# A sliding-window attention block and a mixer MLP on one core: the warm-up reads a tile of zeros, the q and k weights come as two loads, block 3's second norm takes bn_stats, and the whole order is written anew

## The chip, the core and the metric

The kernel runs on one core of a Trainium2 chip, in bf16 with f32 accumulation. The metric is the device time of one launch in microseconds (us). Engines are named as in the profile: PE (TensorE), DVE (VectorE), ACT (ScalarE), POOL (GpSimd) and SP (SyncE, which issues every DMA here).

## The reference, cut to what matters

```python
# S = 2048 rows, D = 448, H = 16 heads of 28, F = 1792
y  = x + A(layernorm(x), wqkv, wo)          # attention
h2 = y + B(layernorm(y), w1, w2, w3, w4)    # mixer and MLP; B normalises its input once more
def A(x, wqkv, wo):
    q, k, v = split(x @ wqkv)               # each row looks at 8 rows: pos, pos-2, ..., pos-14
    logits = einsum("bhsd,bhswd->bhsw", q, k[idx]) * scale      # masked where pos < 0
    return einsum("bhsw,bhswd->bhsd", softmax(logits), v[idx]) @ wo
def B(x, w1, w2, w3, w4):
    h  = gelu(layernorm(x) @ w1)
    hs = concat(4 column groups of h, shifted by +1, -1, +2, -2 rows) @ w2
    x1 = x + hs
    return x1 + gelu(layernorm(x1) @ w3) @ w4
```

## The kernel before

The 2048 rows are four **blocks** of 512 (t = 0 to 3), each of four tiles of 128 rows. The functions `phase_*` record operations, in program order, with the reads and writes of each; nothing is emitted then. Block by block they are:

- **N1**: the first norm. `ln_stats` gives `bn_stats` and `bn_aggr` on DVE (with `STATS` 'a' instead: sums on ACT, by a Copy and a Square that also write out an accumulated sum); `rstd` gives Ln and Exp on ACT; `normalize` writes `lntm`.
- **A1**: the normalised tiles are transposed into `actT` (block 0 by PE transposes against the identity `ident`, tile after tile, in `transposed_single`; later blocks also by DMA), then q and k are computed transposed. `duo` runs two output banks at once on the two halves of the PE rows. The six column groups go in three pairs. **V**: the values, in `vt`, and DMAs that window them into `vw`.
- **A2** and **S**: four products q times shifted k on DVE (`qk_r`: three of 128x4096, one of 128x2048), summed over a head's columns by PE (`zc`), then the softmax: max, subtract, Exp, sum, Ln and Exp for the reciprocal, and `pb`, which PE transposes and ACT copies to `pt` in the arena.
- **A3** and **O**: four products `bd_r` on DVE spread the weights, PE multiplies them with `vw`, copies go to `actT`, and PE multiplies with `wo`; the residual sum replaces `xin`.
- **B1** and **M**: the second norm (twice normalised, so two reciprocal roots), a DMA transpose ("turn"), `w1` and gelu into `gT`.

Then, by units of 2, 4, 4, 4 and 2 tiles: **B2** (`w2` on shifted `gT`, sum on DVE, statistics), **T** (normalise, turn, add x), **W3** (`w3` and gelu, `h3T`) and **B3** (`w4`, sum, store).

What runs when is not decided by these functions. `ORDER` is a list of operation numbers; `arrange` walks it, hands out buffers from small pools (8 PSUM banks, 2 of `qk_r`, 3 of `bd_r`, 4 of `actT`, 2 of `lntm`), and so gives each engine its own queue, which runs strictly in that order. `OTHER` names operations that go to their alternative engine (a copy from ACT to DVE, an addition from POOL to DVE). Waits follow from the recorded reads and writes. ACT holds one table of functions at a time: going from Ln and Exp to gelu or back costs an ACT_TABLE_LOAD in its queue.

Ahead of the data, `warm` gives PE nine matmuls of `ident` with itself; `keep_busy` puts two more between the first transposes. `ident` needs a memset and an affine_select on POOL. In the profile nearly all operations have line L1048 (before) or L1051 (after), where the queues are emitted, so the tile names tell them apart.

## Time and profile before

| what | us |
|---|---|
| median of 3 runs | 189.56 |
| lowest and highest | 188.63, 190.37 |
| the profiled execution | 188.72 |
| its span in the trace | 187.0 |
| PE busy | 180.0 |
| DVE busy | 130.8 |
| ACT busy | 124.0 |

The span begins with the first instruction of the trace and ends with the last; the 1.72 us around it lie outside the trace. Every time given for an instruction is counted from the span's start. A timeline row gives start, length, engine, operation, what is written from what, the count, and in brackets the idle time before it with what ended it. Matmuls are pipelined, so a matmul's length is longer than its share of PE; its share is the distance between starts.

### The profile page before, as it was taken

Reading aid. Unit: us, or ns where it says so; the run is one execution under the profiler, and the core shown is the slowest. Engines: PE = TensorE matmul, PEld = TensorE weight load, DVE = VectorE, ACT = ScalarE, POOL = GpSimd, SP = SyncE. Lnnn points to the kernel's source line nnn. Section 1 sums busy time; section 2 is a strip of 40 time slices with the busy share of each in tenths; the row PEclk is TensorE's granted clock in tenths of the full one; section 3 lists DMA queues with packets and bytes.
Section 4 is the critical chain, followed back from the end, with each engine's and each line's share of the span. In section 5 each row is a group of like instructions: output and inputs, shape, how many; then the busy total and the mean of one; then the engine's idle time right before and its main releaser. Section 6 shows DMA issues by size and latency. Waiting matters only on the chain.

```text
span 187.0 us, 5742 instructions
## 1 busy us (share of the span) xinstructions
PE 180.0 (96%) x2482; PEld 93.5 (50%) x2482; DVE 130.8 (70%) x236; ACT 124.0 (66%) x280; POOL 20.9 (11%) x56
## 2 busy tenths in 40 slices
PE   5999999989999989999999999999999999999994
PEld 2685443345453445467455444555444544555663
DVE  7989999999999999999997960089962080000512
ACT  4459989879999999998991987930267004930340
POOL 3440000000003000500042000020034050000000
PEclk9999999999999999999999999999999999999999
DMA  5923583661654697597409060043305031000022
GB/s 151 340 101 58 125 173 63 141 149 17 115 124 94 160 206 301 100 316 146 101 4 140 2 137 4 0 31 84 100 4 112 4 71 60 4 0 0 4 98 74
DMA packets 38609, 18.29 MB, mean 98 GB/s; under 512 B 27464, under 2 KB 38072, under 8 KB 38584
## 3 DMA queue, kind: packets, MB, share of 16 engines
q1 hardware_dynamic: 38584, 17.93, 41.4%
q8 instruction: 19, 0.31, 0.7%
q14 instruction: 6, 0.05, 0.1%
HBM read 8.14 MB, written 1.84 MB: 53 GB/s over the span
## 4 chain that ended last, share of the span: by engine, by line
PE 75%; DVE 16%; ACT 6%; issue 1%; POOL 0%; POOLq 0%
PE ps L1048 75%; DVE bd_r L1048 6%; DVE qk_r L1048 4%; DVE lntm L1048 2%; ACT lntm L1048 1%; DVE xin L1048 1%; DVE st L1048 1%; ACT arena L1048 1%; DVE mx L1048 1%; ACT h3T L1048 1%; ACT L1048 1%; ACT L1043 1%; DVE arena L1048 1%; ACT xin L1048 1%; DVE pb L1048 0%
## 5 line engine op out<-in xcount | busy, mean ns | idle before, releaser
L1048 PE MATMUL ps<-actT,arena 64*128 64x512 bf16 (+2 forms) x812 | 69.6, 326 | 0.3
L1048 ACT ACTIVATE h3T<-ps 128x512 bf16<-128x512 f32 (+1 forms) x70 | 30.7, 520 | 39.1 <-PE ps L1048 38.7
L1048 PEld LDWEIGHTS ps<-actT,arena 64*128 64x128 bf16 (+1 forms) x812 | 35.7, 96 | 29.8 <-PE ps L1048 1.6
L1048 PE MATMUL ps<-arena,h3T 64*128 64x448 bf16 (+3 forms) x434 | 44.5, 343 | 0.0
L1048 DVE SCALAR_TENSOR_TENSOR ost<-ps,mrs,arena 128x448 bf16<-128x448 f32 (+2 forms) x17 | 10.7, 649 | 35.5 <-PE ps L1048 26.9
L1048 ACT ACTIVATE arena<-ps 128x512 bf16<-128x512 f32 (+4 forms) x62 | 31.5, 568 | 2.6 <-PE ps L1048 2.4
L1048 DVE TENSOR_TENSOR qk_r<-arena 128x4096 bf16<-128x4096 bf16 (+1 forms) x16 | 32.1, 2015 | 0.3 <-PE ps L1048 0.3
L1048 PEld LDWEIGHTS ps<-arena,h3T 64*128 64x128 bf16 (+1 forms) x434 | 22.4, 94 | 19.6 <-ACT h3T L1048 0.3
L1048 DVE TENSOR_TENSOR bd_r<-arena,bmask 80x2048 bf16<-80x2048 bf16 x16 | 18.9, 1211 | 0.3 <-ACT arena L1048 0.3
L1048 DVE TENSOR_SCALAR lntm<-arena,mv,rs_y 128x512 bf16<-128x512 f32 x14 | 6.8, 540 | 13.1 <-ACT rs_y L1048 11.6
L1048 POOL TENSOR_TENSOR arena<-arena,xin 128x448 f32<-128x448 f32 x9 | 10.6, 1193 | 34.3 <-DVE lntm L1048 34.3
L1048 PE MATMUL ps<-wo_s,actT 64*128 64x448 bf16 x128 | 14.3, 350 | 0.1
L1048 PE MATMUL ps<-w_s,arena 64*128 64x448 bf16 x88 | 13.3, 350 | 0.0
L1048 PE MATMUL ps<-actT,w_s 64*128 64x512 bf16 (+1 forms) x112 | 13.3, 376 | 0.0
L1048 ACT ACTIVATE lntm<-xin,nm 128x448 bf16<-128x448 bf16 x16 | 10.5, 660 | 4.0 <-DVE nm L1048 4.0
L1048 ACT ACTIVATE actT<-ps 128x512 bf16<-128x512 f32 (+2 forms) x19 | 11.8, 639 | 2.0 <-PE ps L1048 1.9
L1048 PE MATMUL ps<-arena,actT 64*128 64x448 bf16 x112 | 12.6, 350 | 0.1
L1048 DVE SCALAR_TENSOR_TENSOR arena<-xin,rs_y,ps 128x448 f32<-128x448 bf16 x16 | 10.3, 673 | 0.3 <-PE ps L1048 0.3
L1048 DVE BATCH_NORM_STATS2 st<-xin 128x6 f32<-128x448 bf16 x16 | 9.1, 612 | 0.5 <-DMA xin<-in_A_x_dram 0.4
L1048 ACT ACTIVATE vt<-ps 128x448 bf16<-128x448 f32 x16 | 8.4, 543 | 1.0 <-PE ps L1048 1.0
L1048 PEld LDWEIGHTS ps<-wo_s,actT 64*128 64x128 bf16 x128 | 5.9, 94 | 6.1 <-PE ps L1048 0.9
L1048 PEld LDWEIGHTS ps<-actT,w_s 64*128 64x128 bf16 (+1 forms) x112 | 6.0, 98 | 5.6 <-ACT h3T L1048 0.2
(75 smaller groups left out, 167.1 us busy)
## 6 DMA issues: line engine op xcount, KB each, us to landing
arena<-in_B_w_dram SPq DMA_DIRECT2D x2, 896.0 KB, 7.0
out_dram<-ost SPq DMA_DIRECT2D x15, 112.0 KB, 1.8
arena<-in_B_w_dram SPq DMA_DIRECT2D x2, 784.0 KB, 5.8
vw<-vt SPq DMA_DIRECT2D x4, 320.0 KB, 4.1
vw<-vt SPq DMA_DIRECT2D x4, 256.0 KB, 3.5
arena<-in_A_wqkv_dram SPq DMA_DIRECT2D x2, 448.0 KB, 4.5
xin<-in_A_x_dram SPq DMA_DIRECT2D x2, 448.0 KB, 5.1
xin<-in_A_x_dram SPq DMA_DIRECT2D x3, 224.0 KB, 5.3
```

The costliest lines, as they stand in the source:

```text
L1043: eng.preload_act_table_set("natural_log_exp_and_others")
L1048: inst = getattr(eng, meth)(**kw)
```

## The change

1. POOL first sets a new tile `blank` to zero, and the warm-up and keep-busy matmuls read it in place of `ident`. There are ten warm-up matmuls in place of nine.
2. The load of the q and k columns of `wqkv` (2 DMAs of 448 KB) becomes q, then k (4 DMAs of 224 KB). In block 0 the pairs of column groups are (q0,q1), (k0,k1), (q2,k2) in place of (q0,k0), (q1,k1), (q2,k2).
3. Block 3's second norm takes its sums by `bn_stats` on DVE in place of sums with the residual addition on DVE and Squares on ACT.
4. `ORDER` and `OTHER` are new. By the new `OTHER`, three of block 0's four `actT` copies run on DVE (one before), the two `actT` copies of block 3's attention that ran on DVE go back to ACT, and one addition of unit 2 goes back to POOL.

```diff
-STATS = {'N1': 'vvva', 'B1': 'avaa', 'B2': 'avvvv'}
+STATS = {'N1': 'vvva', 'B1': 'avav', 'B2': 'avvvv'}
...
 OTHER = """
-103 196 198 510 513 564 565 627 629 699 700 701 769 830
+107 110 112 201 203 572 573 637 638 706 709 779 838
 """
-WARM = 9
+WARM = 10
...
+        blank = sb("blank", [128, 128], BF16)
...
+        pool("memset", ap=blank[:], constant=0.0)
         pool("memset", ap=ident[:], constant=0.0)
...
-        load_rows("wqk", wqkv_s[:, :, 0:2 * D], A_wqkv, 0, 2 * D)
+        load_rows("wq", wqkv_s[:, :, 0:D], A_wqkv, 0, D)
+        load_rows("wk", wqkv_s[:, :, D:2 * D], A_wqkv, D, D)
...
-            return mm(busy(), ident[:], bass.AP(ident, 0, [[128, 128], [0, 4], [1, 128]]), True, True, 512, after)
+            return mm(busy(), blank[:], bass.AP(blank, 0, [[128, 128], [0, 4], [1, 128]]), True, True, 512, after)
...
-            names = ("q0", "k0", "q1", "k1", "q2", "k2")
+            names = ("q0", "k0", "q1", "k1", "q2", "k2") if t else ("q0", "q1", "k0", "k1", "q2", "k2")
```

The new `ORDER` moves instructions on every engine. Three places on DVE, as its queue stands in the built programs:

The head of DVE's queue before, from the last setup memset ahead of the first tile: `st<-xin` are the statistics of x, `lntm<-xin` the normalised tiles of block 0, `actT<-ps` the copy of a transposed tile, `vt` and `pb` setup memsets.

```order
L1048 MEMSET pb 128x320
L1048 BN_STATS st<-xin 128x6
L1048 BN_AGGR mv<-st 128x2
L1048 BN_STATS st<-xin 128x6
L1048 BN_AGGR mv<-st 128x2
L1048 TENSOR_SCALAR lntm<-xin,mv,rs_y 128x448
L1048 BN_STATS st<-xin 128x6 x2
L1048 BN_AGGR mv<-st 128x2 x2
L1048 TENSOR_SCALAR lntm<-xin,mv,rs_y 128x448
L1048 MEMSET vt 128x128x2
L1048 TENSOR_SCALAR lntm<-xin,mv,rs_y 128x448 x2
L1048 COPY actT<-ps 128x512
```

And the same place in the changed kernel, up to the statistics of block 1:

```order
L1051 MEMSET vt 128x128x2
L1051 BN_STATS st<-xin 128x6
L1051 BN_AGGR mv<-st 128x2
L1051 BN_STATS st<-xin 128x6
L1051 BN_AGGR mv<-st 128x2
L1051 BN_STATS st<-xin 128x6 x2
L1051 BN_AGGR mv<-st 128x2 x2
L1051 TENSOR_SCALAR lntm<-xin,mv,rs_y 128x448 x4
L1051 COPY actT<-ps 128x512 x3
L1051 MEMSET pb 128x320
L1051 BN_STATS st<-xin 128x6 x2
```

All four tiles' statistics now stand ahead of the first normalised tile, three copies stand where one stood, and the two memsets have changed places.

DVE at the end of block 0's softmax, before: `qk_r` are block 1's products, `ls`, `mx` and `pb` the softmax, `bd_r` the first product of block 0's A3, which needs `pb` transposed by PE and copied by ACT.

```order
L1048 TENSOR_TENSOR ls<-ps,mx 128x512
L1048 TENSOR_TENSOR qk_r<-arena 128x4096
L1048 TENSOR_SCALAR lntm<-xin,nm,rs_y 128x512
L1048 TENSOR_REDUCE mx<-ls 128x64
L1048 TENSOR_SCALAR lntm<-xin,nm,rs_y 128x512 x3
L1048 TENSOR_TENSOR pb<-ls,mx 128x8x64
L1048 TENSOR_TENSOR qk_r<-arena 128x2048
L1048 TENSOR_TENSOR bd_r<-arena,bmask 80x2048
```

The same place in the changed kernel:

```order
L1051 TENSOR_TENSOR ls<-ps,mx 128x512
L1051 TENSOR_SCALAR lntm<-xin,nm,rs_y 128x512 x4
L1051 TENSOR_REDUCE mx<-ls 128x64
L1051 TENSOR_TENSOR qk_r<-arena 128x2048
L1051 TENSOR_TENSOR pb<-ls,mx 128x8x64
L1051 TENSOR_TENSOR qk_r<-arena 128x4096
L1051 TENSOR_TENSOR bd_r<-arena,bmask 80x2048 x2
```

A wide product now stands between `pb` and the first `bd_r`, where a narrow one stood, and four normalisations in place of a wide product stand ahead of the sum over `ls`.

DVE around block 3's A3, before: `st<-arena` are unit 1's statistics, `lntm<-arena` its four normalised tiles (their turn feeds W3 of unit 1), `bd_r` block 3's products, CAST its copies.

```order
L1048 TENSOR_TENSOR pb<-ls,mx 128x8x64
L1048 BN_STATS st<-arena 128x6 x3
L1048 TENSOR_TENSOR bd_r<-arena,bmask 80x2048 x2
L1048 BN_AGGR mv<-st 128x2 x4
L1048 TENSOR_TENSOR bd_r<-arena,bmask 80x2048
L1048 TENSOR_SCALAR rs_x<-mv 128x4
L1048 CAST actT<-ps 128x512
L1048 TENSOR_TENSOR bd_r<-arena,bmask 80x2048
L1048 TENSOR_SCALAR lntm<-arena,mv,rs_y 128x512 x4
L1048 CAST actT<-ps 128x512
```

The same place in the changed kernel:

```order
L1051 TENSOR_TENSOR pb<-ls,mx 128x8x64
L1051 BN_STATS st<-arena 128x6 x2
L1051 BN_AGGR mv<-st 128x2 x4
L1051 TENSOR_SCALAR rs_x<-mv 128x4
L1051 TENSOR_TENSOR bd_r<-arena,bmask 80x2048 x3
L1051 TENSOR_SCALAR lntm<-arena,mv,rs_y 128x512
L1051 TENSOR_TENSOR bd_r<-arena,bmask 80x2048
L1051 TENSOR_SCALAR lntm<-arena,mv,rs_y 128x512 x3
```

All of unit 1's statistics now stand ahead of the first `bd_r`, and the two casts are gone from DVE. On ACT, both copies of block 3's `pb` now stand behind the Ln and Exp of block 2's second norm (one stood ahead of the Ln before), and on PE its transposes stand behind two groups of B3's matmuls where they stood behind one.

60 rows, old and new, of the table ORDER are left out of this document.

## The prediction

> **What bounds the kernel now.** I read the page first, then the busy times by stretch, then the chain that ended last, and last the timeline where the stretches change.
>
> ```profile
> span 187.0 us, 5742 instructions
> PE 180.0 (96%) x2482; PEld 93.5 (50%) x2482; DVE 130.8 (70%) x236; ACT 124.0 (66%) x280; POOL 20.9 (11%) x56
> PE   5999999989999989999999999999999999999994
> DVE  7989999999999999999997960089962080000512
> PEclk9999999999999999999999999999999999999999
> ```
>
> PE looks full and DVE looks idle for a third of the span, but these are averages over two stages: DVE is full up to slice 21 (about 98 us) and loose behind it. The stretches say where the change of hands lies (a row gives the length, then the busy time of PE, PEld, DVE, ACT and POOL, each with its count, the granted clock and the DMA).
>
> ```profile
> 40.00:67.80 27.80, 26.27 (x588) 13.07 (x590) 27.73 (x37) 26.07 (x64) 1.53 (x3) 1.00 0.53 108
> 67.80:85.39 17.59, 17.25 (x239) 9.75 (x240) 17.45 (x33) 17.13 (x38) 2.61 (x3) 1.00 0.74 222
> 85.39:100.00 14.61, 14.61 (x288) 8.33 (x290) 13.30 (x25) 12.49 (x25) 3.29 (x3) 1.00 0.49 97
> 100.00:140.00 40.00, 40.00 (x396) 19.05 (x392) 25.82 (x66) 22.52 (x46) 2.96 (x6) 1.00 0.30 52
> 140.00:184.96 44.96, 44.57 (x480) 24.48 (x476) 9.81 (x17) 15.39 (x35) 5.00 (x4) 1.00 0.17 41
> ```
>
> From 40 to 67.8 us DVE idles 0.07 us and PE 1.53: **DVE decides**. From 67.8 on PE idles 0.34 us, then nothing, and 0.39 in the last stretch: **PE decides**. The last real waits of PE are these two, for block 2's A3 product and for block 0's gelu:
>
> ```profile
> 66.96 0.42 PE L1048 MATMUL ps<-bd_r,vw 80*32 80x64 bf16 x32 [0.52 <-DVE bd_r L1048]
> 67.78 0.35 PE L1048 MATMUL ps<-w_a,arena 64*128 64x448 bf16 x1 [0.40 <-ACT arena L1048]
> ...
> 85.39 99.20 PE ps L1048 x1158
> ```
>
> The last row is from the chain: one unbroken run of PE, 99.2 us long, ends the kernel. The new order puts the same matmuls ahead of that point as the old one (all of block 0 to 2's attention, B2 of units 0 and 1, W3 of unit 0) and the same behind it. So the result is a sum of two terms: by how much DVE's queue comes earlier or later to 67 us, and what PE newly waits for behind it.
>
> **The head.** PE first, then DVE:
>
> ```profile
> 2.09 4.02 PE L1048 MATMUL ps<-ident 128*128 128x512 bf16 x9 [2.09 <-POOL ident L1048]
> 5.91 0.63 PE L1048 MATMUL ps<-ident,lntm 128*128 128x128 bf16 x4
> 7.61 0.86 PE L1048 MATMUL ps<-ident,lntm 128*128 128x128 bf16 x8
> 8.40 5.32 PE L1048 MATMUL ps<-actT,arena 64*128 64x256 bf16 x100
> 2.19 0.99 SPq L1048 DMA_DIRECT2D arena<-in_A_wqkv_dram  x2
> 1.39 0.20 POOL L1048 MEMSET ident<- 128x128 bf16 x1
> ...
> 2.47 0.33 DVE L1048 MEMSET pb<- 128x320 uint32 x1
> 2.90 0.63 DVE L1048 BATCH_NORM_STATS2 st<-xin 128x6 f32<-128x448 bf16 x1
> 4.29 0.18 DVE L1048 BATCH_NORM_AGGREGATE mv<-st 128x2 f32<-128x6 f32 x1
> 4.41 0.40 DVE L1048 TENSOR_SCALAR lntm<-xin,mv,rs_y 128x448 bf16<-128x448 bf16 x1
> 6.36 0.27 DVE L1048 MEMSET vt<- 128x256 uint32 x1
> 6.68 1.10 DVE L1048 TENSOR_SCALAR lntm<-xin,mv,rs_y 128x448 bf16<-128x448 bf16 x2
> 7.70 0.41 DVE L1048 COPY actT<-ps 128x512 bf16<-128x512 bf16 x1
> 8.52 0.63 DVE L1048 BATCH_NORM_STATS2 st<-xin 128x6 f32<-128x448 bf16 x1 [0.41 <-DMA xin<-in_A_x_dram]
> ```
>
> The warm-up waits for `ident`. With `blank` as POOL's first instruction (0.20 us from 0.80, where POOL's first memset starts) PE begins at about 1.05 us, 1.04 earlier. Nine warm matmuls took 5.91 - 2.09 = 3.82, so ten take 4.25, to 5.3. That alone moves nothing: before, the first tile was normalised by 4.81 (4.41 + 0.40) and waited 1.1 us for PE to leave the warm-up. Now DVE does the statistics of all four tiles first. From 4.47, where the second aggregate ends, two more bn_stats with overlap (1.15), two aggregates (0.30) and one normalisation (0.40) give 6.2. The wait has changed sides: PE idles from 5.3 to 6.2, and the transposes start 0.3 later than at 5.91. The split load adds two DMA issues of 0.5 us (0.99 for two) ahead of block 1's x, which landed at 8.5; at worst it lands at 9.5, the same as the late end below. The first matmuls that read a weight start at 8.40 and read q alone.
>
> What counts is when DVE gets to block 1's statistics, 8.52 before. Its queue now holds two more copies of 0.41; `vt` (0.27) has moved into the free time ahead of 2.90, and `pb` (0.33) has moved out of it, ahead of block 1. The third and fourth transposes bind the copies. How late depends on PE's rate, which doubles in this stretch: 0.42 us for 512 columns in the warm-up, but 5.32 / 50 = 0.106 for 256 (two at once) from 8.40. The granted clock reads 9 (90% or more) throughout, so only the distances show it. The doubling came by about 8.1, six us after PE's first matmul. If it stays at 8.1, the four transposes and two keep-busy matmuls at the old rate end at about 8.6, copies run to 9.2, `pb` to 9.5: block 1's statistics are **0.9 late**. If it comes before 6.2, the last normalisation binds instead: the pair that took 1.10 us from 6.68 now starts about 0.2 earlier and ends at 7.6, copies end at 8.7, `pb` at 8.85: **0.3 late**. Six us after PE's first matmul would now be 7.1, and by that I take **+0.5**.
>
> The Trainium skill ("TensorE: Matmul & The Clock Gate", Part 1) says that PE starts at half clock and goes to full after one busy window of about 3.4 us, and that the windows run freely. The trace agrees with the halves (0.42 against 0.21 for 512 columns) and not with the page's other figure, about 4 us into activity: here it was 6. By the window, the rate would double anywhere between 4.5 and 7.9 (an estimate from that page), and the term would be +0.3 to +0.9, the same bounds.
>
> **The order up to 67 us.** DVE's work from block 1's statistics to block 2's residual sum is the same list of operations. What differs are its idle times:
>
> ```profile
> 11.61 1.31 DVE L1048 TENSOR_SCALAR lntm<-xin,mv,rs_y 128x448 bf16<-128x448 bf16 x4 [0.60 <-ACT rs_y L1048]
> 21.25 3.43 DVE L1048 TENSOR_TENSOR qk_r<-arena 128x4096 bf16<-128x4096 bf16 x2 [0.26 <-PE ps L1048]
> 25.09 0.17 DVE L1048 TENSOR_SCALAR nm<-mv 128x4 f32<-128x4 f32 x1 [0.42 <-ACT lntm L1048]
> 25.17 2.29 DVE L1048 TENSOR_TENSOR qk_r<-arena 128x4096 bf16<-128x4096 bf16 x1
> 35.48 1.22 DVE L1048 TENSOR_TENSOR qk_r<-arena 128x2048 bf16<-128x2048 bf16 x1
> 37.03 1.22 DVE L1048 TENSOR_TENSOR bd_r<-arena,bmask 80x2048 bf16<-80x2048 bf16 x1 [0.33 <-ACT arena L1048]
> 15.99 0.60 SPq L1048 DMA_DIRECT2D xin<-in_A_x_dram  x1
> ```
>
> The first wait (0.60) stays: statistics, Ln and Exp, normalisation follow each other as before. The one at 21.25 was a wait for a product buffer whose matmuls stood far back in PE's queue; they now start when the second product ends, before the third needs the buffer: gone. The one at 25.09 waited for block 3's sums on ACT, whose x came by a DMA that SP issued at 15.99 behind a halo copy; that load now goes out with the others, and ACT has these sums earlier in its queue: gone. The one at 37.03 was the way from `pb` through PE and ACT to the first `bd_r`, covered by a narrow product of 1.22 us; a wide one of 2.29 covers it now, so it is gone. Together 1.01. New waits can come where four normalisations now stand ahead of the sum over `ls`, which needs ACT's Exp: walking ACT's queue with its own rows I find the Exp done within 0.1 to 0.3 of when DVE gets there. I take **-0.8**, with -1.0 (all gone) and 0 (all come back elsewhere) as the ends.
>
> **Behind 67 us.** The extra matmul is in the head. Block 3's statistics: four Squares leave ACT, four bn_stats and aggregates come to DVE:
>
> ```profile
> 102.83 0.67 ACT L1048 ACTIVATE lntm<-xin,nm 128x448 bf16<-128x448 bf16 x1 [3.84 <-DVE nm L1048]
> L1048 DVE BATCH_NORM_STATS2 st<-xin 128x6 f32<-128x448 bf16 x16 | 9.1, 612 | 0.5 <-DMA xin<-in_A_x_dram 0.4
> 89.49 2.33 DVE L1048 TENSOR_TENSOR bd_r<-arena,bmask 80x2048 bf16<-80x2048 bf16 x2
> 97.45 1.98 SPq L1048 DMA_TRANSPOSE actT<-lntm  x1
> 103.01 10.75 PE L1048 MATMUL ps<-actT,arena 64*128 64x512 bf16 x98
> 107.94 1.89 SPq L1048 DMA_TRANSPOSE actT<-lntm  x1
> ```
>
> Squares cost 4 x 0.65 = 2.6 us on an ACT that had idled 3.84; bn_stats and aggregates cost DVE about 4 x 0.53 + 0.4 = 2.5 with overlap, two of them while the last residual sums wait for PE. The turn that follows went out at 107.94; I get 107.4 for the new one. PE has W3 of unit 1 to do from 103.01 for 10.75 us, so this is worth **0** either way; without that cover it would be the 0.5. The addition given back to POOL and the casts given to ACT lie beside full PE too.
>
> The tight place is W3 of unit 1 at 103.01: its turn went out at 97.45. In the new order block 3's `pb` is transposed one B3 group later (14 matmuls, about 1.3 us), and both copies stand behind a table load, so the first `bd_r` starts at about 90.7 in place of 89.49, and DVE idles about 0.9 ahead of it. DVE no longer does two casts there, and the fourth normalisation of unit 1 ends at about 97.0, 0.4 before the old one. So **0** again, with +0.6 as the end if the copies on ACT come late for O.
>
> **Sum:** +0.5 - 0.8 + 0 + 0 = -0.3 on the profiled execution's 188.72 us (span 187.0 and 1.72 around it): 188.4. That execution was 0.84 under the median 189.56, so on the median the forecast is **189.3**; its own range, from the bounds, is +0.9 + 0 + 0.6 = +1.5 and +0.3 - 1.0 = -0.7: 188.9 to 191.1.
>
> **The rivals.** 1% is 1.9 us here, and about what a measurement can tell, since the three runs lie 1.74 apart.
>
> *The early start carries.* PE's rate doubles before the first transposes, all 1.01 us of idle time go, and PE's remaining 0.73 us of waits from 67.8 on go too: 0.3 - 1.0 - 0.7 = -1.4, 188.2. For it: PE does start a full us earlier. Against: DVE, not PE, has the next word at 6.2, and a shorter head than 8.52 is shut out by its own copies. That the change doesn't do what its warm-up says is thus already in the forecast.
>
> *The gap shuts the gate.* PE idles from 5.3 to 6.2, which it did not before. If the idle time sends the count back to the first transpose, the rate doubles six us behind 6.2, at 12.2; block 0's q and k matmuls from about 8.8 then run 3.4 us at half rate and lose 1.7. Copies of k, block 1's transposes and ACT's queue behind them come that much later, while DVE has 2 us of block 2's statistics to do meanwhile; of the +0.9 and 1.7 some 2.1 reach DVE's first products, less 0.8: +1.3, 190.9. It decides if the rate is still halved at 9 us.
>
> *Block 3's A3 comes too late (slower).* The kernel is slower if its first `bd_r` starts later than about 91.1: then unit 1's normalisation passes 97.45, and PE has no other work before W3 of unit 1. One more ACT table load ahead of the copies, or the same for O's copies, is 1.3 us, and the normalisation and O each lie on that way: +1.3 to +2.6, about 191.6. For it: 0.4 us of slack, and three chains (Ln and Exp, `pb`, unit 1's statistics) that must all hold. Against: each was walked with its own rows.
>
> **How the numbers follow.** Forecast 0.50, early start 0.18, gate 0.12, late A3 0.16, something that I do not see 0.04, even to both sides. Over 1% faster (under 187.7) takes half of the early start and half of the unseen: 0.11. Over 1% slower (above 191.5) takes three quarters of the late A3, a third of the gate and half of the unseen: 0.18. Within 1%: 0.71. The range leaves out the lower half of the early start and the upper half of the late A3: 187.6 to 191.9.
>
> **What would show it.** In the changed profile: PE's first matmul at about 1.05 and its first wait at 5.3 for `lntm`; DVE's fifth bn_stats, the first of block 1, at 8.8 to 9.5; no idle time before the third product and before block 0's first `bd_r`; that `bd_r` at 36.4 to 37.3; a wait of 0.5 to 1.3 us before block 3's; W3 of unit 1 starting within 0.6 of 102.7, and PE unbroken from 85 on. The prediction is wrong if PE waits anywhere behind 70 us for more than 1 us, or if DVE idles more than 2 us between 12 and 67.

## The result, and the profile after

| | before | after |
|---|---|---|
| median of 20 runs | 189.47 | 191.29 |
| lowest, highest | 188.38, 190.37 | 189.83, 193.79 |
| the profiled execution | 188.72 | 190.76 |
| its span | 187.0 | 189.0 |

The ratio is 1.0095, with a 95% interval of 1.0076 to 1.0115: the change makes the kernel **slower by 1%**, where 0.1% faster was forecast. The runs also lie wider apart, 3.96 us from lowest to highest in place of 1.99. In 5 of the 20 executions the mean granted clock of TensorE was 0.991, and these are the five slowest (192.28 to 193.79); the other 15 have a median of 190.90. Of before, all of the runs that were made beside the experiments below had 0.999 or 1.000. (The ratio leaves out executions more than 1.5% above the fastest, two of the five among them.)

The first rows of the page after: span, PE and DVE in 40 slices, and the granted clock of the profiled execution.

```profile
span 189.0 us, 5737 instructions
PE 179.9 (95%) x2483; PEld 93.5 (49%) x2483; DVE 131.5 (70%) x239; ACT 121.2 (64%) x272; POOL 22.9 (12%) x58
PE   7799999999879989999999899999999999999994
DVE  7989999999998999999898960077966032000503
PEclk9999999999999999999999999999999999999999
```

Busy times over the whole span are those of before within 3 us on every engine; what the 2.0 us are made of shows stage by stage. PE has an 8 and a 7 in its eleventh and twelfth slices (47 to 57 us) and an 8 in its twenty-third (104 to 109) where it had 9. Two of the stretches of before, in the same columns:

```profile
40.00:67.80 27.80, 24.91 (x524) 12.16 (x518) 26.59 (x36) 25.07 (x61) 4.07 (x3) 1.00 0.51 105
100.00:140.00 40.00, 39.24 (x390) 18.70 (x388) 25.30 (x61) 19.05 (x36) 3.06 (x6) 1.00 0.26 55
```

From 40 to 67.8 us DVE, which decides there, idles 1.21 us in place of 0.07. From 100 to 140 PE, which decides there, idles 0.76 in place of nothing. To see how much each stage costs, I read the start of the same operation in both timelines. These are the rows of after, by time:

```profile
1.05 4.26 PE L1051 MATMUL ps<-blank 128*128 128x512 bf16 x10 [1.05 <-POOL blank L1051]
6.37 0.38 PE L1051 MATMUL ps<-ident,lntm 128*128 128x128 bf16 x4 [1.06 <-DVE lntm L1051]
8.94 1.08 DVE L1051 BATCH_NORM_STATS2 st<-xin 128x6 f32<-128x448 bf16 x2
36.70 2.36 DVE L1051 TENSOR_TENSOR bd_r<-arena,bmask 80x2048 bf16<-80x2048 bf16 x2
64.47 4.62 DVE L1051 TENSOR_TENSOR bd_r<-arena,bmask 80x2048 bf16<-80x2048 bf16 x4
68.77 0.35 PE L1051 MATMUL ps<-w_a,arena 64*128 64x448 bf16 x1 [0.35 <-ACT arena L1051]
105.11 1.25 PE L1051 MATMUL ps<-actT,arena 64*128 64x512 bf16 x10 [0.76 <-DMA actT<-lntm]
```

and the one of before that the prediction did not need:

```profile
63.42 4.62 DVE L1048 TENSOR_TENSOR bd_r<-arena,bmask 80x2048 bf16<-80x2048 bf16 x4
```

| up to | before | after | lost in this stage |
|---|---|---|---|
| DVE: block 1's first bn_stats | 8.52 | 8.94 | +0.42 |
| DVE: block 0's first `bd_r` | 37.03 | 36.70 | -0.75 |
| DVE: block 2's four `bd_r` | 63.42 | 64.47 | **+1.38** |
| PE: B2 of unit 0 | 67.78 | 68.77 | -0.06 |
| PE: W3 of unit 1 | 103.01 | 105.11 | **+1.11** |
| end of the span | 187.0 | 189.0 | -0.1 |

**First place, 42 to 59 us.** DVE's new waits, then what ACT and PE do there:

```profile
42.88 0.69 DVE L1051 TENSOR_REDUCE mx<-ls 128x64 f32<-128x512 f32 x1 [0.36 <-ACT ls L1051]
57.50 0.63 DVE L1051 BATCH_NORM_STATS2 st<-xin 128x6 f32<-128x448 bf16 x1 [0.26 <-ACT xin L1051]
58.64 0.69 DVE L1051 TENSOR_REDUCE mx<-ps 128x64 f32<-128x512 f32 x1 [0.51 <-PE ps L1051]
...
41.73 0.60 ACT L1051 ACTIVATE actT<-ps 128x512 bf16<-128x512 f32 x1 [1.32 <-PE ps L1051]
42.23 0.62 ACT L1051 ACTIVATE ls<-ls 128x512 f32<-128x512 f32 x1
...
51.98 0.70 PE L1051 MATMUL ps<-bd_r,vw 80*32 80x64 bf16 x64
53.23 0.32 PE L1051 MATMUL ps<-bd_r,vw 80*32 80x64 bf16 x18 [0.55 <-DVE bd_r L1051]
54.35 0.29 PE L1051 MATMUL ps<-bd_r,vw 80*32 80x64 bf16 x14 [0.79 <-issue]
54.57 0.93 PE L1051 MATMUL ps<-wo_s,actT 64*128 64x448 bf16 x8
```

Three waits of DVE, 1.13 us, answer to three that went (1.01); the other 0.24 of this stage is busy time of DVE itself (26.56 us in place of 26.32). The first wait comes from ACT's queue: block 1's `ls` is there at 41.39, but a copy to `actT`, which waits 1.32 us for PE's A3 pass, stands ahead of its Exp, so that this starts at 42.23 (in the old order at 40.62, ahead of the copy). The second and third hang on block 1's O group, which now starts at 54.57. It stands behind all four A3 passes of block 1 (32 small matmuls each), the last three of them in a row. PE runs out of work there: it waits 0.55 for the fourth `bd_r`, and then, in the middle of that pass, 0.79 "issue", for nothing that the profile shows. In the old order V and k products of later blocks stood between the first three, and O's first group ran ahead of the last:

```profile
52.98 0.42 PE L1048 MATMUL ps<-bd_r,vw 80*32 80x64 bf16 x32
53.34 0.93 PE L1048 MATMUL ps<-wo_s,actT 64*128 64x448 bf16 x8
54.39 0.42 PE L1048 MATMUL ps<-bd_r,vw 80*32 80x64 bf16 x32
```

**Second place, 91 to 105 us.** Block 3's first `bd_r`, unit 1's last normalisations, three DMA issues of SP ahead of unit 1's turn, and the turn, for which W3 (quoted above) waits 0.76; the last row is of before:

```profile
91.98 3.49 DVE L1051 TENSOR_TENSOR bd_r<-arena,bmask 80x2048 bf16<-80x2048 bf16 x3 [0.76 <-ACT arena L1051]
96.98 1.45 DVE L1051 TENSOR_SCALAR lntm<-arena,mv,rs_y 128x512 bf16<-128x512 f32 x3
95.77 3.14 SPq L1051 DMA_DIRECT2D arena<-arena  x3
98.97 1.97 SPq L1051 DMA_TRANSPOSE actT<-lntm  x1
...
94.80 2.13 SPq L1048 DMA_DIRECT2D arena<-arena  x3
```

This turn goes out 1.52 later than at 97.45. Of these, 0.99 were there at 68.77 already, and they are no part of this stage's +1.11, since PE's own work starts later by the same 0.99. The stage adds 0.53, and not on DVE: although block 3's first `bd_r` waits, unit 1's last normalisation ends 29.66 us behind the start of B2 of unit 0, in place of 29.64. The turn is held by **SP's queue**. Three copies `arena<-arena`, two columns at the edge of block 2's `gT` each, stand ahead of it and follow ACT's gelus of block 2; their issue ends at 98.91, 0.48 behind the last normalisation (98.43). Before, it ended at 96.93, and the turn waited for the normalisation (97.42).

Its way to PE took 6.10 us (the chain has "98.97 6.10 DMA actT<-lntm") where the old one took 5.5, as the DMA view of before shows for 97 to 103.5 us:

```profile
actT<-lntm SPq DMA_TRANSPOSE x1, 5.5
```

97.45 + 5.5 is 102.95, and the old W3 started at 103.01. So the old kernel had next to no slack there (the view rounds to 0.1 us): its turn arrived just in time. The waits are not the whole of the +1.11: from B2 of unit 0 to W3 of unit 1 PE idles 1.04 us in place of 0.34, and is busy 35.30 in place of 34.89 with as many matmuls (556 and 557 records).

### The profile page after: what moved, and what is told of

It is laid out like the page before. It is cut to its first block, busy times and chain, and to the rows that moved or that the text cites. A ratio compares the mean times of both kernels' runs of the same rounds, so it can differ in the third digit from the quotient of the medians.

```text
span 189.0 us, 5737 instructions
## 1 busy us (share of the span) xinstructions
PE 179.9 (95%) x2483; PEld 93.5 (49%) x2483; DVE 131.5 (70%) x239; ACT 121.2 (64%) x272; POOL 22.9 (12%) x58
## 4 chain that ended last, share of the span: by engine, by line
PE 76%; DVE 9%; DMA 8%; ACT 4%; issue 1%; SPq 0%
PE ps L1051 76%; DMA actT<-lntm 6%; DVE qk_r L1051 2%; DVE bd_r L1051 2%; ACT arena L1051 2%; DVE lntm L1051 2%; DMA xin<-in_A_x_dram 2%; ACT L1051 1%; DVE arena L1051 1%; DVE st L1051 1%; ACT vt L1051 1%; SPq L1051 0%; DVE ost L1051 0%; DVE mx L1051 0%; DVE pb L1051 0%
## 5 line engine op out<-in xcount | busy, mean ns | idle before, releaser
L1051 PE MATMUL ps<-actT,arena 64*128 64x512 bf16 (+2 forms) x812 | 68.7, 325 | 0.9 <-DMA actT<-lntm 0.8
L1051 PEld LDWEIGHTS ps<-actT,arena 64*128 64x128 bf16 (+1 forms) x812 | 36.2, 96 | 30.4 <-PE ps L1051 1.8
L1051 DVE SCALAR_TENSOR_TENSOR ost<-ps,mrs,arena 128x448 bf16<-128x448 f32 (+2 forms) x17 | 10.6, 653 | 35.7 <-PE ps L1051 35.6
L1051 ACT ACTIVATE rs_x<-mv,epsilon 128x4 f32<-128x4 f32 (+2 forms) x16 | 4.7, 297 | 12.8 <-DVE mv L1051 12.7
L1051 ACT ACTIVATE actT<-ps 128x512 bf16<-128x512 f32 (+2 forms) x19 | 11.3, 636 | 1.8 <-PE ps L1051 1.8
L1051 DVE BATCH_NORM_STATS2 st<-xin 128x6 f32<-128x448 bf16 x20 | 11.5, 608 | 0.5 <-ACT xin L1051 0.3
```

The costliest lines, as they stand in the source:

```text
L1051: inst = getattr(eng, meth)(**kw)
```

## The experiments

Fourteen kernels, each with a profile and 6 or 12 timed executions beside the kernel before. "0.991" counts the executions with that mean clock; the last four columns are of the profiled execution. The fifth is the stage of the first place; B2 of unit 0 always starts 4.30 to 4.36 us behind block 2's first `bd_r`.

| run | ratio (95% interval) | 0.991 | block 0's first `bd_r` | from there to block 2's | B2 of unit 0 | from there to W3 of unit 1 |
|---|---|---|---|---|---|---|
| before | 1 | none | 37.03 | 26.39 | 67.78 | 35.23 |
| the change | 1.0095 (1.0076 to 1.0115) | 5 of 20 | 36.70 | 27.77 | 68.77 | 36.34 |
| old_order | 1.0189 (1.0133 to 1.0245) | 3 of 6 | 37.33 | 26.39 | 68.08 | 35.49 |
| old_order_2 | 1.0087 (1.0060 to 1.0114) | 0 of 6 | 37.18 | 26.39 | 67.93 | 35.31 |
| new_to_37 | 1.0190 (1.0137 to 1.0243) | 3 of 6 | 38.28 | 27.26 | 69.88 | 35.30 |
| new_to_67 | 1.0208 (1.0170 to 1.0247) | 0 of 6 | 36.77 | 27.48 | 68.56 | 36.49 |
| new_from_67 | 1.0024 (0.9995 to 1.0054) | 2 of 12 | 37.04 | 27.00 | 68.39 | 35.72 |
| warm_13 | 1.0059 (1.0027 to 1.0091) | 3 of 12 | 36.66 | 27.24 | 68.20 | 35.88 |
| o_before_a3 | 1.0102 (1.0069 to 1.0135) | 0 of 6 | 37.11 | 27.29 | 68.71 | 36.41 |
| pb_earlier | 1.0142 (1.0102 to 1.0182) | 1 of 6 | 36.66 | 28.07 | 69.04 | 36.91 |
| late_warm | 1.0103 (1.0054 to 1.0152) | 3 of 6 | 37.45 | 29.77 | 71.53 | 35.77 |
| early_alone | 1.0018 (0.9993 to 1.0043) | 1 of 12 | 37.01 | 26.97 | 68.33 | 35.25 |
| new_old_new | 1.0050 (1.0027 to 1.0073) | 0 of 12 | 37.40 | 27.43 | 69.18 | 35.89 |
| new_then_old | 1.0020 (0.9993 to 1.0046) | 1 of 12 | 36.77 | 27.18 | 68.30 | 35.28 |
| both_gaps | 1.0040 (1.0020 to 1.0060) | 0 of 12 | 37.10 | 27.28 | 68.68 | 35.81 |
| both_gaps_turns | 1.0096 (1.0073 to 1.0119) | 0 of 6 | 37.09 | 27.28 | 68.67 | 36.88 |

From the start of W3 of unit 1 to PE's end it is 81.5 to 81.6 us in before, after and every kernel whose W3 of unit 1 runs through. So the last two columns hold the whole difference between profiled executions.

### Old and new order by halves

All four have every edit of the change (zeros, ten warm matmuls, split load, bn_stats); only the order differs. An order of before is carried over operation by operation.

```diff
-ORDER = new
+ORDER = before                                  (old_order)
+ORDER = new up to block 0's first bd_r, then before    (new_to_37)
+ORDER = new up to block 2's last bd_r, then before     (new_to_67)
+ORDER = before up to block 2's last bd_r, then new     (new_from_67)
```

> All edits of the change (early warm-up on zeros, ten warm matmuls, weights as q then k, bn_stats for block 3), but every engine in the order of before. Theory 'order': the 2.0 us come from the new order, 1.0 ahead of 67 us and 1.0 behind it; then this kernel stands within 0.4 us of before (ratio 0.998 to 1.002). Rival 'parts': the edits cost the time by themselves (PE idle at 5.3, two more loads ahead of block 1's x, bn_stats on VectorE); then it is 1.5 to 2 us slower (ratio 1.008 to 1.010).

> The changed program in the new order up to block 0's first masked product on VectorE (36.7 us), from there in the order of before. Theory 'order': at this point VectorE was 0.33 us ahead of before, and the old order has no idle time between 37 and 67, so this kernel is 0.3 us faster than before (ratio 0.996 to 1.000). Rival 'parts': 1.5 to 2 us slower.

> The new order up to block 2's last masked product (67 us), the old one from there. Theory 'order': the three waits that came back in VectorE's queue between 42 and 59 are in it, the late turn behind 67 is not: +1.0 at 67 us, +0.8 to +1.0 at the end (ratio 1.004 to 1.006). If the waits in front do not count and only the part behind 67 does: no change.

> The old order up to block 2's last masked product (67 us), the new one from there. Theory 'order': block 2's turn, block 3's transposes of pb and unit 1's turn come late without any delay in front: +0.8 to +1.2 (ratio 1.004 to 1.007). If these are late only because VectorE is already 1.0 behind at 67 us: no change.

The first three came out 1.9 to 2.1% slow, which neither theory had. The reason was how I had placed block 3's bn_stats in the old order: each directly behind its residual sum on DVE, ahead of the four sums of unit 1 that empty product buffers. PE's timeline of old_order, W3 of unit 1:

```profile
105.47 1.04 PE L1051 MATMUL ps<-actT,arena 64*128 64x512 bf16 x8 [0.86 <-DVE xin L1051]
107.74 9.02 PE L1051 MATMUL ps<-actT,arena 64*128 64x512 bf16 x82 [1.23 <-DVE arena L1051]
```

0.86 and 1.23 are waits for DVE to empty a bank, so these three say little on the order. new_from_67, whose bn_stats stand where the change has them, is the clean one: with the old order up to 67 us the change costs 0.2% in place of 1%, and less than the 0.8 to 1.2 us expected of it. **Most of the loss comes from the new order ahead of 67 us.** Its second half by itself is later by 35.72 - 35.23 = 0.5.

The old order is not free of loss ahead of 67 us either. From block 0's first `bd_r` to block 2's it takes 26.39 us in before, old_order and old_order_2, but 27.00 in new_from_67. There PE stalls in the middle of a group of matmuls on `actT`, block 0's O and the transposes of block 1's `pb` come later, and DVE waits for the copies of these:

```profile
43.42 0.82 PE L1051 MATMUL ps<-actT,arena 64*128 64x512 bf16 x6 [0.54 <-issue]
...
46.73 1.22 DVE L1051 TENSOR_TENSOR bd_r<-arena,bmask 80x2048 bf16<-80x2048 bf16 x1 [0.47 <-ACT arena L1051]
```

new_from_67 and old_order have the same order there, so this stall comes in some executions and not in others; the last section returns to it.

new_to_37 showed something else. Its TensorE timeline of the head, and the granted clock (the number before the last two) in half microseconds around 109 to 113 us:

```profile
7.24 0.63 PE L1051 MATMUL ps<-ident,lntm 128*128 128x128 bf16 x4
7.66 0.63 PE L1051 MATMUL ps<-blank 128*128 128x512 bf16 x1
...
109.00:109.50 0.50, 0.00 (x0) 0.00 (x0) 0.50 (x2) 0.50 (x1) 0.00 (x0) 0.89 0.00 0
110.00:110.50 0.50, 0.50 (x6) 0.22 (x4) 0.50 (x2) 0.00 (x0) 0.00 (x0) 0.50 0.00 0
112.50:113.00 0.50, 0.50 (x6) 0.25 (x4) 0.50 (x2) 0.24 (x1) 0.00 (x0) 0.69 0.00 0
```

Four transposes take 0.42 us from 7.24 (half rate); in the changed kernel's profile they take 0.22 from 6.81. Here the rate doubled only at 10.3, by the distances of the q and k matmuls, 9.2 us after PE's first matmul (6.0 in before). And at 109.4 (0.89 over the half microsecond) the clock was halved until 112.8 (0.69): **3.4 us at 0.50**, behind waits of 1.07 and 1.23 us among which PE worked for one. Such a stretch takes 1.7 us of clock, 0.9% of the span: that is the mean of 0.991. So idle time of PE can bring half clock, in some executions and not in others: in the profile of old_order the waits of 0.86 and 1.23 left the clock at 1.00.

### The two idle stretches of PE

`warm_13` fills the head's gap, `o_before_a3` takes the pass that stalls out of the row, `both_gaps` does both.

```diff
-WARM = 10
+WARM = 13
```

> The changed kernel with 13 warm matmuls in place of 10, so that TensorE has work until the first normalised tile is there (10 took 4.26 us and left it idle for 1.06). Theory 'gate': in one execution of the experiment new_to_37 TensorE's rate doubled only at 10.35 us, after an idle stretch of 0.93 at 5.5, and there a stretch of half clock 3.4 us long (109.4 to 112.8) followed 2.3 us of idle time; so the idle time at 5.3 delays the doubling, or brings half clock back, in some executions. Without it: no execution with a mean clock of 0.991 (5 of 20 had it), a spread of 2 us in place of 4, and a median 0.4 to 0.8 us lower (ratio 1.004 to 1.007). Rival: the 0.991 come from idle time later on (53 or 104 us); then their share stays and the ratio stays at 1.009.

PE's timeline of warm_13: the first transposes, and the four passes.

```profile
6.34 0.38 PE L1051 MATMUL ps<-ident,lntm 128*128 128x128 bf16 x4 [0.32 <-DVE lntm L1051]
...
53.19 0.30 PE L1051 MATMUL ps<-bd_r,vw 80*32 80x64 bf16 x15 [0.55 <-DVE bd_r L1051]
53.77 0.31 PE L1051 MATMUL ps<-bd_r,vw 80*32 80x64 bf16 x17 [0.28 <-issue]
```

The median (189.89) stands 0.73 us above that of before in the same rounds (189.16), in place of 1.82: 1.1 us less, more than expected, though the intervals of the two ratios overlap. Of the nine executions at full clock eight lie between 189.38 and 190.11. In the changed kernel 7 of the 15 lie from 189.83 to 190.76 and 8 from 190.90 to 192.16. That fits a rate that doubles early in some executions and late in the others, once the gap is there; one profile each (after, new_to_37) shows the two cases, and that they are the two groups is argued from the spread, not profiled one by one. The two profiled executions do not show it: in both the rate had doubled before 6.4 and block 1's statistics started at 8.94 and 8.91. The 1.0 us between their spans comes later, 0.53 between block 0's and block 2's `bd_r`, where the stall is 0.28 in place of 0.79, and 0.46 ahead of W3 of unit 1. So a shorter stall is a rival to the filled gap, and no run tells the two apart. The share of 0.991 stayed, 3 of 12: the rival was right on this half. The issue stall is there again, and three matmuls earlier in the pass (15 ahead of it, not 18): three more warm matmuls, three fewer here. It stands at a fixed **count of PE's instructions**, not at an operation: in all five kernels that have it here, 853 or 854 matmuls stand ahead of it.

```diff
 MATMUL ps<-bd_r,vw x64
+MATMUL ps<-wo_s,actT x8
+MATMUL ps<-xin,ident x2
 MATMUL ps<-bd_r,vw x32
-MATMUL ps<-wo_s,actT x8
-MATMUL ps<-xin,ident x2
```

> The changed kernel with one move on TensorE: block 1's first O group (10 matmuls) ahead of the last of its four A3 passes, as before. Theory 'front': O then starts at 53.6 in place of 54.6, VectorE's waits of 0.26 (at 57.5) and 0.51 (at 58.6) go, and 67 us come 0.8 earlier: ratio 1.004 to 1.006. Rival: VectorE's queue is late for another reason, or what is gained is lost at unit 1's turn: ratio 1.008 to 1.010.

```profile
54.04 0.93 PE L1051 MATMUL ps<-wo_s,actT 64*128 64x448 bf16 x8 [0.94 <-ACT actT L1051]
```

The stall is gone, but O now waits 0.94 for the copies of its own input on ACT and starts at 54.04. No gain in the median (190.75, 1.59 above before in the same rounds; the change's runs at full clock stand 1.43 above it): as an account of the time the front theory was too simple, since O's start hangs on ACT as well. In the profile the stage itself is 0.48 shorter than the change's (27.29 in place of 27.77), but block 1's statistics started 0.42 later (9.36), behind a load of x. But none of its runs was at 0.991.

The change with its warm-up on `ident`, as before:

```diff
-            return mm(busy(), blank[:], bass.AP(blank, 0, [[128, 128], [0, 4], [1, 128]]), True, True, 512, after)
+            return mm(busy(), ident[:], bass.AP(ident, 0, [[128, 128], [0, 4], [1, 128]]), True, True, 512, after)
```

> The changed kernel with its warm-up on the identity tile, as before, so that TensorE starts about 1.3 later (2.36) and its ten warm matmuls end at about 6.6, just after the first normalised tile (6.37): no idle time, no early start. Theory 'gate': the idle stretch of 1.06 is what delays the doubling in some executions, the early start itself is worth nothing, since VectorE sets the pace: median as warm_13 (full-clock runs 0.8 to 1.2 us under the changed kernel's; ratio 1.002 to 1.007). If the runs with a mean clock of 0.991 come from a rate that doubles early and is halved again in the idle stretch, none of these has it; if they come from idle time later on, their share stays at 1 in 4. Rival: the early start helps in itself: slower than warm_13 by 0.5 or more.

PE started at 2.38, the rate doubled at 8.3, and block 1's statistics started at 9.77, 0.83 later than in the change. The time misses what was expected: its three executions at full clock have a median of 190.59, 0.3 under the change's and 0.9 above warm_13's (189.70), so here the rival had the sign. This kernel has no gap in the head, and 3 of 6 executions were at 0.991; one of them was profiled. PE, DVE and the granted clock (the number before the last two) around its four A3 passes:

```profile
53.99 0.33 PE L1051 MATMUL ps<-bd_r,vw 80*32 80x64 bf16 x19 [0.56 <-DVE bd_r L1051]
55.55 0.29 PE L1051 MATMUL ps<-bd_r,vw 80*32 80x64 bf16 x13 [1.23 <-issue]
55.77 1.37 PE L1051 MATMUL ps<-wo_s,actT 64*128 64x448 bf16 x8
60.24 0.63 DVE L1051 BATCH_NORM_STATS2 st<-xin 128x6 f32<-128x448 bf16 x1 [2.25 <-ACT xin L1051]
...
55.00:56.00 1.00, 0.45 (x17) 0.31 (x19) 1.00 (x3) 0.52 (x2) 0.00 (x0) 1.00 0.29 61
56.00:57.00 1.00, 1.00 (x10) 0.38 (x6) 1.00 (x1) 1.00 (x2) 0.83 (x1) 0.56 0.08 16
58.00:59.00 1.00, 1.00 (x8) 0.37 (x6) 0.00 (x0) 0.00 (x0) 1.00 (x2) 0.50 0.00 0
59.00:60.00 1.00, 1.00 (x10) 0.49 (x8) 0.00 (x0) 0.33 (x1) 0.69 (x2) 0.73 0.77 151
```

PE idles 0.56 + 1.23 = 1.79 us within 2.1, the clock is halved from 56.1 to 59.5, O takes 1.37 for eight matmuls where it took 0.93, and DVE waits 2.25 for its sums where it had waited 0.26. In this kernel, then, the half clock comes from this place.

`both_gaps` has the edits of warm_13 and of o_before_a3:

```diff
-WARM = 10
+WARM = 13
...
+MATMUL ps<-wo_s,actT x8
+MATMUL ps<-xin,ident x2
 MATMUL ps<-bd_r,vw x32
```

> The changed kernel with both idle stretches of TensorE closed: 13 warm matmuls (as warm_13) and block 1's first O group ahead of its last A3 pass (as o_before_a3). Theory 'gate': half clock comes for 3.4 us in the executions in which the idle time among the A3 passes (0.55 + 0.3 to 1.2) empties a window of the clock's count, as the profile of late_warm shows (clock 0.66 from 55 to 60, VectorE waiting 2.25 at 58); with the pass moved it has no such stretch: no execution of 12 at 0.991 (warm_13 had 3), median 189.4 to 189.8, ratio 1.001 to 1.004. Rival: the half clock has another place: 2 to 4 executions at 0.991.

None of 12 at 0.991, a spread of 1.44 us, a ratio of 1.0040. The three kernels in which the pass is moved have 0 of 24, the five with the last three passes in a row (the change, new_to_67, warm_13, pb_earlier, late_warm) 12 of 50. So the half clock of the changed kernel most likely comes from this place: if the 12 fell at random among the 74, all would miss the 24 with a chance of about one in two hundred. It is not shown outright, since none of the change's own five was profiled and new_to_67, with the three passes in a row, has 0 of 6. Where it comes from in the 4 of 36 executions of early_alone, new_from_67 and new_then_old, which have the old order here, no profile shows.

### Behind 67 us

`pb_earlier`, on PE and ACT, and with two bn_stats behind `pb` on DVE:

```diff
+MATMUL ps<-arena,h3T x14
+MATMUL ps<-ident,pb x16
 MATMUL ps<-arena,h3T x28
-MATMUL ps<-ident,pb x16
-MATMUL ps<-arena,h3T x14
...
+ACTIVATE arena<-ps 80x512 x2
 ACT_TABLE_LOAD
 ACTIVATE rs_x<-mv,epsilon
 ACTIVATE rs_y<-rs_x
-ACTIVATE arena<-ps 80x512 x2
```

> The changed kernel with block 3's second pb transposed 14 matmuls earlier on TensorE, two bn_stats behind pb on VectorE, and pb's two copies ahead of the table load on ScalarE, as before. Theory 'back': block 3's first masked product starts at about 91.1 in place of 91.98, unit 1's turn goes out at about 98.1 in place of 98.97, and the wait of 0.76 ahead of W3 of unit 1 goes: 0.7 us, ratio 1.005 to 1.007. Rival: the turn is late because everything is 1.0 late at 67 us, and something else takes the place: no change.

`both_gaps_turns` adds to both_gaps the same and, on DVE:

```diff
-SCALAR_TENSOR_TENSOR arena<-xin,rs_y,ps x3
+SCALAR_TENSOR_TENSOR arena<-xin,rs_y,ps
 TENSOR_SCALAR lntm<-xin,nm,rs_y x4
+SCALAR_TENSOR_TENSOR arena<-xin,rs_y,ps x2
```

> As both_gaps, with block 3's pb, its transposes and copies earlier (as pb_earlier), and block 2's four normalisations ahead of two of unit 1's sums on VectorE, as before, so that M2's turn goes out about 1.2 earlier. Theory 'back': in pb_earlier the fourth masked product waited 0.62 for TensorE, because M2's matmuls stood ahead of block 3's first A3 pass and waited for their turn; with both mended the time from unit 1's first B2 matmul to the end falls from 117.4 to 117.9 to that of before (116.8): 0.5 to 1 us faster than both_gaps, ratio 0.996 to 1.000. Rival: unit 1's turn is held by VectorE's own queue (no casts left to take out): the same time as both_gaps.

Neither gained. A row of DVE of pb_earlier, then one of PE of both_gaps_turns:

```profile
96.21 1.22 DVE L1051 TENSOR_TENSOR bd_r<-arena,bmask 80x2048 bf16<-80x2048 bf16 x1 [0.62 <-PE ps L1051]
...
86.72 2.27 PE L1051 MATMUL ps<-actT,arena 64*128 64x256 bf16 x34 [1.05 <-DVE arena L1051]
```

In the first the fourth `bd_r` waits 0.62 for PE, and the turn goes out at 99.73; in the second the four normalisations hold up two sums that empty product buffers, and W3 of unit 0 waits 1.05 for them. From B2 to W3 both took 36.9 us, longer than the change. And neither moved what holds the turn: in all nine kernels with the new order behind 67 us it goes out 0.04 to 0.07 us behind SP's issues of the copies at block 2's edge, and 0.26 to 0.93 behind the last normalisation; in the seven with the old one, 0.02 to 0.03 behind the last normalisation and 0.5 behind the copies. In both experiments the copies came later still (by 0.5 and 1.2 us, counted from B2 of unit 0). What is shown is the size: 35.2 to 35.3 where the order of before runs there with its sums on ACT (before, early_alone, new_then_old), 35.7 to 36.4 where the new one does (the change, new_from_67, warm_13, o_before_a3, late_warm, new_old_new, both_gaps). Of the half microsecond in new_from_67, whose W3 of unit 1 does not wait for the turn, 0.41 is busy time of PE (35.30 in place of 34.89). Which single move makes it is open.

### The parts alone

```diff
 SCALAR_TENSOR_TENSOR arena<-xin,rs_y,ps x4
+BN_STATS st<-xin x4
+BN_AGGR mv<-st x4
```

> As old_order (all edits, order of before), but block 3's bn_stats stand behind the four sums of unit 1 on VectorE. In old_order they stood ahead of these, the sums released their product buffers late, and W3 of unit 1 waited 0.21 + 0.86 + 1.23 = 2.3 us. Theory 'order': these 2.3 go, what is left of the edits is the head (block 1's statistics 0.35 to 0.65 later) and the gate's late doublings: ratio 1.000 to 1.006. Rival 'parts': above 1.009.

These waits went, and another came, in W3 of unit 1:

```profile
110.53 1.80 PE L1051 MATMUL ps<-actT,arena 64*128 64x512 bf16 x14 [1.08 <-ACT h3T L1051]
...
107.55 0.30 ACT L1051 ACTIVATE rs_x<-mv,epsilon 128x4 f32<-128x4 f32 x1 [8.40 <-DVE mv L1051]
```

ACT's Ln waits for the last aggregate (107.55), and W3's gelus stand behind it. So in the old order four bn_stats cost 2.1 us (0.86 and 1.23) ahead of unit 1's sums and 1.1 behind them; in the new order, which puts them between, PE does not wait for them: "block 3's statistics are hidden" holds for their place, not for themselves.

```diff
+        pool("memset", ap=blank[:], constant=0.0)
-            return mm(busy(), ident[:], bass.AP(ident, 0, [[128, 128], [0, 4], [1, 128]]), True, True, 512, after)
+            return mm(busy(), blank[:], bass.AP(blank, 0, [[128, 128], [0, 4], [1, 128]]), True, True, 512, after)
```

> The kernel before with one edit: its nine warm matmuls and keep-busy matmuls read a tile of zeros that is written first, so that TensorE starts at 1.05 in place of 2.09. Theory 'gate': no gain, since VectorE's fifth bn_stats waits for its data until 8.5 anyway; but TensorE now idles between the first transposes (from 4.9) and the second tile (6.4), the doubling comes late in some executions, and the spread grows: ratio 1.000 to 1.004. Rival: the early start alone is worth up to 1 us: ratio 0.995 to 0.999.

Starting PE a microsecond earlier is worth nothing: 1.0018, the interval holds 1. Block 1's statistics started at 8.79 (8.52 before), so DVE was not served earlier; at block 0's first `bd_r` it was level with before (37.01), and the 0.58 that it lost up to block 2's came with the same stall as in new_from_67 (it ends at 43.38 here).

The last two have the late warm-up of late_warm and halves of both orders:

```diff
-ORDER = new
+ORDER = new up to block 0's first bd_r, before up to block 2's last, then new    (new_old_new)
+ORDER = new up to block 0's first bd_r, then before; STATS B1 'avaa'             (new_then_old)
```

> The changed kernel with the late warm-up of late_warm, the new order up to 36.7 us, the old one from there to 67, the new one behind. Theory: the three old waits (1.01 us) are gone, the three new ones (1.13) and TensorE's stall among block 1's A3 passes (0.3 to 1.1) too; what is left against before is block 1's later start (0.4 to 0.6) and unit 1's later turn (0.4): ratio 0.999 to 1.003. If the new order behind 67 costs a full microsecond by itself: 1.005.

> As new_old_new, but from 36.7 us on everything as before, block 3's sums of squares on ScalarE again (no bn_stats there). Unit 1's turn then costs nothing new: ratio 0.997 to 1.001. If the change's first stage is worth nothing either: 1.002 or more.

new_old_new is 0.5% slow: its late warm-up moved block 1's statistics to 9.72, and the new order behind 67 costs its 0.7 (35.89 against 35.23). new_then_old is level with before (1.0020, the interval holds 1). That does not mean that the three waits taken out of DVE's queue up to 37 us are worth nothing: although block 1 started 0.58 later (9.10), block 0's first `bd_r` came 0.26 earlier than before (36.77), and 0.79 was lost after it, in the order of before. Part of that is made by the seam: block 0's O waits 0.40 for the load of `wo` in new_then_old and 0.69 in new_old_new, a wait that neither whole order has, and PE stalls ahead of it as in new_from_67. So these two do not settle what the first stage is worth. No version was faster than the kernel before.

## Why the prediction was wrong

The time, 191.29, lies within the range of 187.6 to 191.9, near its upper end, and the ratio of 1.0095 just inside the 1% that had 0.71. But a gain of 0.1% was forecast, and the measured change is a loss, with an interval (1.0076 to 1.0115) wholly beyond 1. That the range holds it is luck: its upper end came from the rival of the late A3, and most of the loss arose ahead of that. The prediction's own signs of being wrong did not show either: PE waited 0.76 behind 70 us (over 1 was the sign), DVE idled 1.53 from 12 to 67 (over 2). In its rivals, two shares do not follow from their own times: the early start stands at 188.2, but half of it was counted as under 187.7, and the late A3, 190.9 to 192.2, has about half above 191.5, not three quarters.

**The head, +0.5: right in the profiled execution, too small in others.** PE began at 1.05 and first waited at 5.3 for `lntm` (1.06, to 6.37); block 1's statistics started at 8.94, +0.42. But late_warm, whose rate doubled at 8.3, much as in before (8.1), started them at 9.77: +1.25, not the +0.9 that I gave for a late doubling. And in both_gaps the rate had doubled before 6.30, yet they started at 9.49, held 0.55 by the load of x: the 9.5 that I had named as the worst of the split load.

**The gap shuts the gate, a rival at 0.12: open.** In the profiled execution the rate doubled before 6.37; in new_to_37, with the same head, at 10.3. I had priced this at 190.9 and one place. I treated the doubling as one time that holds for all executions, and it moves from one to the next. That the gap is what moves it is argued: the kernel with the gap filled has a median 1.1 us lower, but its stall is shorter too.

**The order up to 67 us, -0.8: this is the step that failed.** Up to block 0's first `bd_r` it is right: -0.75, the three waits gone but for 0.16 at 25.05, that `bd_r` at 36.70 (36.4 to 37.3 forecast). Then +1.38 came back by 64.5, and the bounds of -1.0 to 0 had no room for it. I counted the idle times that vanish and looked for new ones at one place, block 0's sum over `ls`; in ACT's queue the Exp of block 1's `ls` then stood behind a copy that waits for PE (0.36). And I took DVE's 0.07 us of idle time from 40 to 67.8 as a property of that stage, when it hung on PE's queue: in the old order the fillers between the A3 passes kept O and the next sums on time. The passes in a row stood in the new order, and I did not walk them. The old order in this stage loses 0.00 to 0.61 where nothing else is moved (old_order, old_order_2, early_alone, new_from_67), the new one 0.85 to 1.68 at full clock. Moving O ahead of the last pass does not restore it (0.90): the part of the stall is about 0.5, and the rest of the +1.38 was not undone by any single move.

**Behind 67 us, 0, with +0.6 as the end: measured +1.01** (1.11 up to W3 of unit 1, 0.1 regained by the end). The wait ahead of block 3's `bd_r` was there (0.76; 0.5 to 1.3 forecast). I had unit 1's turn go out 0.4 earlier than before, when its last normalisation ends. Counted from B2 of unit 0, the normalisation ended when it had before (29.66, 29.64) and the turn went out 0.53 later, behind SP's copies for block 2, whose queue I did not walk; on its way it took 0.6 longer, for a reason that no run shows. The old turn landed at 102.95 for a start at 103.01, so nothing covered that. The rival *block 3's A3 comes too late*, at 0.16 and +1.3 to +2.6, named the place and its point (a first `bd_r` later than 91.1; it was 91.98), but not the way: its late normalisation is not what held the turn. A term that I put at nothing, the matmuls' own time, is 0.41 of the 1.11.

**Not foreseen: the half clock**, most likely behind PE's idle time among the A3 passes, 5 of 20 executions, 1.7 us each (192.64, the median of these five, against 190.90).

So on the profiled execution: +0.42 - 0.75 + 1.38 - 0.06 + 1.01 = +2.0, against the forecast's +0.5 - 0.8 + 0; and the median of 20 is another 0.53 above that execution, for effects that come and go.

## What to carry to other kernels

When an order is rewritten, the idle times that the old one had are the smaller half of the sum: walk the queues of the engines that *serve* the critical one, SP's DMA issues too, through the whole stage, since its lack of idle time is their merit. Compare stages from a common start: lateness that all engines bring along is not lost a second time. Before a chain is taken as covered, compare when its data land with when they are used; 0.06 us between the two is no cover. And keep TensorE's small matmuls mixed with long ones: a row of short passes, each waiting for its data, cost first their own waits, then a stall, then, in 12 of 50 executions here, the clock.

## What was not expected of the hardware

**Half clock returns after less than 2 us of idle time.** In late_warm, 1.79 us of idle time were enough to halve the clock for 3.4 us; in new_to_37, 2.3. In the changed kernel's profile 0.55 + 0.79 = 1.34 were not, nor were 0.86 + 1.23 in old_order's or 0.78 + 1.23 in new_to_67's, where the clock stayed at 1.00: the sum of idle time alone does not decide. The Trainium skill ("TensorE: Matmul & The Clock Gate", Part 1) tells of free-running windows of about 3.4 us and a return to half clock after an idle window; the length agrees with both stretches (56.1 to 59.5, 109.4 to 112.8), but no window here was wholly idle: of the 3.4 us ahead of 56.1 PE had worked 1.6, of those ahead of 109.4 it had worked 1.3. The granted clock reads 1.00 through the head, where the distances show half rate, so a mean clock of 1.000 says nothing of the first ten microseconds.

**PE can stall with nothing to wait for.** In the five kernels that keep the three passes in a row the same stall came, 15 to 19 matmuls into the last pass. Against the start of a 16 KB transfer on the instruction queue (read in windows of 0.2 us):

| | transfer starts | stall | PE goes on |
|---|---|---|---|
| warm_13 | 50.8 | 0.28 | 53.77 |
| new_to_67 | 51.0 | 0.50 | 54.14 |
| the change | 51.8 | 0.79 | 54.35 |
| pb_earlier | 52.2 | 1.10 | 54.62 |
| late_warm | 53.2 | 1.23 | 55.55 |

The row of that queue for 51.8 to 52.0 us in the changed kernel (count, MB, share):

```profile
q8 instruction: 1, 0.02, 28.8%
```

PE goes on 2.3 to 3.1 us after the transfer starts, and the later it starts, the longer the stall. The order of before has such a place too: in five of the seven experiments that have it from 37 to 67 us (early_alone, new_from_67, new_to_37, new_old_new, new_then_old), 600 or 601 matmuls stand ahead of a stall, and PE goes on 2.4 to 2.9 us after a transfer starts (41.0 and 43.42 in new_from_67). In before, old_order and old_order_2 that transfer started at 40.2, PE passed the point at 42.8 to 43.1, and nothing was lost. That PE had run through its instructions and waited for the next block is the reading that fits; no run changed the transfer itself, so it is not shown. The Trainium skill ("Runtime: NRT & Kernel Launch", Instruction fetch mechanics) says that instructions come in 16 KiB blocks by a queue of the engine's own, and that the cost of crossing a block is mostly hidden. The size agrees (0.31 MB in 19 transfers here); hidden it was in most places, and not behind the 82 short matmuls, and as many weight loads, that run just ahead of the stall in the change, nor always in the old order, where 32 short ones and a dozen longer run ahead of that place.
